# A kernel whose instruction order comes from a planner: the planner is given other transfer times, other mode-change times and a new table of keys

## The chip, the cores and the metric

The kernel runs on one core of one Trainium2 chip. The metric is the device time of one execution in microseconds (us), the median of several executions; lower is better. The engines are named as in the profile: PE is the matmul engine, PEld its weight loads, DVE the vector engine, ACT the scalar engine, POOL the GpSimd engine, SP the engine that issues most DMAs.

## The reference, cut to what matters

Two steps, in float32 (the weights may arrive as float64): a gated linear attention with a complex decay for 4 batches x 8 heads, 768 steps, head size 48, and a feed-forward layer with a softplus on its output.

```python
mag = np.sqrt(a_re * a_re + a_im * a_im)
scale = np.minimum(mag, 0.999) / (mag + 1e-06)
for t in range(S):                     # 768 steps, per batch and head
    S_re, S_im = ar * S_re - ai * S_im + k_t v_t^T, ar * S_im + ai * S_re
    y[:, :, t] = q_t @ S_re
x = y.transpose(0, 2, 1, 3).reshape(3072, 384)
h = x @ w_in                           # 384 -> 2048
g = np.maximum(h, 0.0) + np.log1p(np.exp(-np.abs(h)))
out = g @ w_out                        # 2048 -> 384
```

## The kernel before

**Attention.** The recurrence is done in chunks of 128 steps. The 24 chunks (6 time groups x 4 batches) are prepared in 14 slices: the first time group has one slice for each batch, every later group two slices of two batches. `pre` turns the decays of a slice into a running log magnitude and a running angle: on ACT logarithms and exponentials (one function table) and arctangent, sine and cosine (another table, and each change of table is an ACT_TABLE_LOAD from line 1031), on DVE products, and for the first time group the running sums as matmuls (L596). L668 and L670 then rotate keys and queries by cosine and sine. `chunk` moves the rotated block by four DMAs from one place in SBUF to another, into the tile qk (L717, L721), computes scores in 32-row pieces (L787), masks them on DVE (L791), adds the part of the carried state (L820) and the part within the chunk (L823), splits the result into a high and a low part in xt (L832 on ACT or L831 on DVE, then L833), and updates the state (L736 transposes, L743 and L745 copies, L859 matmuls, L871).

**Feed-forward.** `moe` takes one time group (512 tokens) at a time. For each of 16 blocks f of the inner size it runs nine matmuls into h (L898: three blocks of the input size, each as high x high, low x high, high x low), the softplus on ACT (L903, L904, L905) and DVE (L914, for the first group L908), the split of g (L916 on DVE or L917 on ACT, and L918), and two blocks later nine matmuls into the three accumulators o (L934). In the first group the second product is done with unsplit float32 weights (L931, three matmuls). The weights are loaded as 16 tiles raw_wi and raw_wo (L392, 768 KB each), converted from float64 words on DVE (L402, L405, L409) and split (L416 to L419).

**Order.** Nothing is scheduled by hand. Every task is entered with an engine, an assumed duration, its inputs and outputs, its buffers and a key (a due time). `Planner.order` plays the program through once: whenever an engine is free, it takes the ready task with the lowest key whose buffers are free. ACT tasks that need the other function table are put back by `tpen`, PE tasks in the other matmul mode (32-row pieces against full 128 rows) by `mpen`, and some ACT or DVE tasks may go to the other engine. When PE has nothing ready before the first feed-forward result, a filler matmul on the identity matrix is put in (L972). What the planner emits is each engine's instruction order; at run time every engine runs its list strictly in that order and waits where an input is missing. The keys come from the table K (base keys for each slice, chunk, weight and time group, and `nudge`, which shifts single tasks).

The lines on which the planner's clock of a DMA rests:

```python
if e == "SP":
    dma_free = max(dma_free, now + dur + 0.65) + t.nbytes / 330e3
    t.end = dma_free + 2.0
```

Of the kernel before, what the change touches and what calls it, by code (L numbers as in the profile page):

```python
# [21 lines left out]
P = 128  # L22
B, H, S, D = 4, 8, 768, 48
# [3 lines left out]
NI = DM // P  # L27
# [7 lines left out]
QT = 32  # L35
NQ = P // QT
# [52 lines left out]
class Task:  # L89
    __slots__ = ("eng", "dur", "fn", "key", "idx", "deps", "outs", "bufs", "tab", "nbytes", "left", "ready", "end", "alt", "mode")  # L90

    def __init__(self, eng, dur, fn, key, idx, tab, nbytes, mode=0):
        self.mode = mode
        self.eng, self.dur, self.fn, self.key, self.idx, self.tab, self.nbytes = eng, dur, fn, key, idx, tab, nbytes
        self.deps, self.outs, self.bufs, self.end = set(), [], [], 0.0
        self.alt = {}


class Planner:
    WIN = 3.4133  # L100
    FREE = 0.2
    SWITCH = (0.13, 0.095)
# [27 lines left out]
    def add(self, eng, dur, fn, key, r=(), w=(), tab=None, nbytes=0, mode=0):  # L130
        t = Task(eng, dur, fn, key, len(self.tasks), tab, nbytes, mode)
# [17 lines left out]
    def order(self, filler, until, gate):  # L149
# [44 lines left out]
        while done < n:  # L194
            for x in [x for x in ends if x[0] <= now]:
# [3 lines left out]
                for b in t.bufs:  # L199
                    users[b] = users.get(b, b.users) - 1  # L200
                    if users[b] == 0:
                        freed.append((t.end + self.FREE, b))
# [12 lines left out]
            for e in engines:  # L215
# [25 lines left out]
                if best is None and e == "PE" and ends and gate.end and not until.end:  # L241
                    t = Task("PE", FILL, filler, 0, -1, None, 0)
                    free[e] = now + self.array(now, t.dur + (self.SWITCH[0] if mode else 0.0))
# [59 lines left out]
class Prog:  # L303
# [165 lines left out]
    def pre(self, si):  # L469
# [60 lines left out]
        for j, w in enumerate((ca, sa)):  # L530
            def load(j=j):
# [6 lines left out]
            add("SP", 0.45, load,  # L538
                k + 0.1 * j, w=w, nbytes=8 * W * P)
# [139 lines left out]
    def chunk(self, si, c):  # L679
# [44 lines left out]
        for y in range(2):  # L724
            add("SP", 0.62, lambda y=y: heads(y), at(), r=rs, w=[(room, y)], nbytes=2 * D * NI * 1024)
        for y in range(2):
            add("SP", 0.62 if y else 1.4, lambda y=y: shared(y), at(), r=rs, w=[(room, 2 + y)], nbytes=2 * D * 1024)
# [23 lines left out]
        if not last and turned:  # L751
# [21 lines left out]
            add("SP", 2.0, back, at("state"), r=[kd], w=[k2], nbytes=5 * NQ * NI * 2 * QT * P)  # L773
# [366 lines left out]
    def tokens(self):  # L1140
# [73 lines left out]
        -16.338, 5181.86, 176.442, 1628.366, 68.743, 2476.615, 12057.262, 8932.26, 4865.317, 9147.526,  # L1214
        5423.692, 9290.079, 7158.223, 2244.123,
    ],
    "turn": [
        1592.16, 14330.158, 926.506, 1114.172, 2002.13, 8009.243, 7280.747, 7229.777, 2074.974, 18289.305,
        16766.682, 6503.433, 8105.153, 20021.708,
    ],  # L1220
    "tail": [
        226.025, 7990.761, 6717.881, 21069.729, 17662.929, 591.778, 3489.081, 3529.209, 2603.006, 18343.569,
        4472.776, 15471.677, 5298.621, 9447.507,
    ],
    "chunk": [
        -5948.126, 4596.693, 15086.453, 18259.591, 4231.75, 278.86, 1826.896, 2584.494, 518.594, 19365.021,
        1532.72, 14660.162, 6114.859, 22685.821, 7987.101, 4607.589, 20075.365, 7820.913, 15476.253,
        15113.712, 5780.716, 3707.156, 9835.409, 9278.805,
    ],
    "state": [  # L1230
        -17713.56, -25296.17, -5912.358, -1072.654, 80.456, 83.211, 122.678, 99.685, 129.906, 130.2, 154.062,
        147.079, 239.946, 176.388, 309.671, 460.52, 627.645, 901.311, 1502.438, 1822.573, 5296.098, 16265.588,
        19931.86, -586.874,
    ],
    "wgt": [
        13.204, 635.646, 440.261, 16753.966, 17898.824, 3564.011, 16258.655, 1674.662, 16642.242, -12846.499,
        710.902, 8004.565, 9718.573, 17872.114, 15509.821, 13690.111,
    ],
    "low": [
        3706.381, 13481.854, 4674.202, 518.67, 12581.252, 18757.155, -457.641, 127.016, 9766.312, 7691.499,  # L1240
        10533.41, 1633.717, 889.978, 19008.362, 16824.551, 16699.959,
    ],
    "moe": [
        51.097, 100.548, 355.358, 850.441, 4520.98, 22694.101,
    ],
    "step": [
        2.766, 4.919, 22.222, 144.776, 1126.208, 24756076.64,
    ],
    "seen": 22461.439,
    "seenstep": 0.268,  # L1250
    "rlead": 7551.755,
    "xlead": -7696.933,
    "vlead": -2102.967,
    "backlog": 1.748,
    "mpen": 0.622,
    "altpen": 0.065,
    "tpen": 1.84,
    "table": 1.3,
    "nudge": {
# [87 lines left out]
```

## Time and profile before

| | us |
|---|---|
| median of 3 executions | 575.77 |
| lowest and highest | 575.57, 577.8 |
| profiled execution: span from first to last instruction | 573.5 |
| PE busy | 543.3 (95%) |
| DVE busy | 438.9 (77%) |
| ACT busy | 422.9 (74%) |
| POOL busy | 5.7 (1%) |

The profile gives the span of one execution and not that execution's own full time; the median stands 2.3 us above the span. "Busy" for PE means that some matmul is in flight. A wait is put down to what came last before it ended; "issue" is time for which the profile shows no releaser.

### The profile page before, as it was taken

The numbers are of one execution on the slowest core, as the hardware profiler recorded it, in microseconds if no ns is written. First come the engines' busy times: TensorE is split into PE (matmuls) and PEld (weight loads), VectorE is DVE, ScalarE is ACT, GpSimd is POOL, SyncE is SP. The second block draws the span as 40 slices with busy tenths as digits, with TensorE's granted clock in tenths as the row PEclk, the third lists the DMA queues.
The fourth block names the chain that finished last, engine by engine and source line by source line (L and its number), as shares of the span: only waits on it lengthen the run. The fifth ranks groups of instructions, "written<-read, shape, count | busy, mean of one in ns | idle before, by whom it ended". The sixth has DMA issues, their size and how long they took to land.

```text
span 573.5 us, 14092 instructions
## 1 busy us (share of the span) xinstructions
PE 543.3 (95%) x5902; PEld 430.8 (75%) x5902; DVE 438.9 (77%) x681; ACT 422.9 (74%) x728; POOL 5.7 (1%) x27
## 2 busy tenths in 40 slices
PE   0998899999989999999999999999999999999995
PEld 0987766566667888878878887878878888888874
DVE  6598799999787999988899896886987544444442
ACT  7972688878579899786795966774969899854442
POOL 3000000000000000000000000000000000000000
PEclk9999999999999999999999999999999999999998
DMA  8869930162644413457276338184076887210002
GB/s 312 361 163 286 404 149 0 39 188 56 155 156 106 148 32 98 158 135 230 55 183 194 99 95 234 25 219 137 17 183 199 264 249 224 74 56 0 0 2 58
DMA packets 50164, 82.36 MB, mean 144 GB/s; under 512 B 4400, under 2 KB 34352, under 8 KB 50096
## 3 DMA queue, kind: packets, MB, share of 16 engines
q1 hardware_dynamic: 49568, 81.15, 47.2%
q8 instruction: 47, 0.77, 0.6%
q10 hardware_dynamic: 528, 0.26, 0.2%
q14 instruction: 21, 0.17, 0.1%
HBM read 54.66 MB, written 7.86 MB: 109 GB/s over the span
## 4 chain that ended last, share of the span: by engine, by line
PE 82%; ACT 7%; DVE 5%; issue 3%; DMA 2%; SPq 0%; DVEq 0%; ACTq 0%
PE h L898 32%; PE o L934 25%; PE o L931 7%; PE att L787 5%; PE att L820 3%; PE att L823 3%; PE o L972 3%; PE att L859 2%; DMA x<-dense_dram 2%; ACT L1031 1%; PE att L736 1%; DVE lt L914 1%; PE y L823 1%; ACT t L628 0%; ACT t L632 0%
## 5 line engine op out<-in xcount | busy, mean ns | idle before, releaser
L898 PE MATMUL h<-xt,wi 128*128 128x512 f32 x864 | 220.8, 402 | 1.1 <-DVE lt L914 0.9
L898 PEld LDWEIGHTS h<-xt,wi 128*128 128x128 f32 x864 | 160.0, 188 | 42.8 <-issue 3.9
L934 PE MATMUL o<-gh,wo 128*128 128x512 f32 x480 | 160.9, 396 | 0.0
L914 DVE SCALAR_TENSOR_TENSOR lt<-h,lt 128x512 f32<-128x512 f32 x80 | 54.7, 688 | 77.0 <-ACT lt L905 76.7
L903 ACT ACTIVATE lt<-h 128x512 f32<-128x512 f32 x96 | 56.5, 592 | 74.1 <-PE h L898 70.6
L934 PEld LDWEIGHTS o<-gh,wo 128*128 128x128 f32 x480 | 90.1, 188 | 21.6 <-issue 0.8
L934 PE MATMUL o<-gl,wo 128*128 128x512 f32 x240 | 94.3, 393 | 0.0
L905 ACT ACTIVATE lt<-lt,fixed 128x512 f32<-128x512 f32 x96 | 68.7, 719 | 1.6
L904 ACT ACTIVATE lt<-lt 128x512 f32<-128x512 f32 x96 | 59.9, 628 | 1.9
L918 DVE TENSOR_TENSOR gl<-lt,gh 128x512 fp32r<-128x512 f32 x80 | 54.6, 688 | 2.9 <-ACT gh L917 1.4
L934 PEld LDWEIGHTS o<-gl,wo 128*128 128x128 f32 x240 | 45.1, 188 | 10.1
L931 PE MATMUL o<-gf,raw_wo 128*128 128x512 f32 x96 | 43.7, 594 | 0.0
L1031 ACT ACT_TABLE_LOAD x30 | 38.5, 1283 | 0.5
L791 DVE TENSOR_TENSOR a<-att,mask 128x512 f32<-128x512 f32 x48 | 30.9, 682 | 9.3 <-PE att L787 9.2
L787 PE MATMUL att<-qk 96*32 96x96 f32 (+3 forms) x1536 | 33.3, 234 | 4.6 <-issue 4.6
L575 DVE TENSOR_TENSOR_SCAN t<-hold,t 128x384 f32<-128x384 uint8 x40 | 36.1, 945 | 0.7
L787 PEld LDWEIGHTS att<-qk 96*32 96x32 f32 x1536 | 29.7, 110 | 9.1 <-issue 7.3
L917 ACT ACTIVATE gh<-lt 128x512 fp32r<-128x512 f32 x30 | 18.7, 628 | 16.5 <-DVE lt L914 15.8
L931 PEld LDWEIGHTS o<-gf,raw_wo 128*128 128x128 f32 x96 | 17.8, 189 | 17.2 <-issue 15.8
L972 PE MATMUL o<-ident 128*128 128x128 f32 x196 | 25.9, 279 | 0.0
L916 DVE TENSOR_SCALAR gh<-lt 128x512 fp32r<-128x512 f32 x50 | 21.2, 425 | 5.8 <-PE o L934 2.5
L972 PEld LDWEIGHTS o<-ident 128*128 128x128 f32 x196 | 23.8, 193 | 0.9 <-issue 0.6
(102 smaller groups left out, 678.1 us busy)
## 6 DMA issues: line engine op xcount, KB each, us to landing
x<-dense_dram SPq DMA_DIRECT2D x20, 768.0 KB, 6.6
qk<-x SPq DMA_DIRECT2D x48, 288.0 KB, 4.1
raw_wo<-w_out_dram SPq DMA_DIRECT2D x8, 768.0 KB, 11.2
raw_wi<-w_in_dram SPq DMA_DIRECT2D x8, 768.0 KB, 9.5
seen<-w_in_dram SPq DMA_DIRECT2D x16, 384.0 KB, 3.9
seen<-w_out_dram SPq DMA_DIRECT2D x16, 384.0 KB, 4.3
v<-vpad_dram SPq DMA_DIRECT2D x24, 224.0 KB, 4.0
qk<-x SPq DMA_DIRECT2D x48, 96.0 KB, 3.8
```

Of the source, the lines that this page charges most:

```text
L575: V.tensor_tensor_scan(out()[:, s], self.hold, inc()[:, s], 0.0, ALU.mult, ALU.add)
L787: PE.matmul(psc()[QT * u : QT * (u + 1), hh * P + f : (hh + 1) * P], q[:, h, CH + f : CH + f + QT], q[:, h, f:CH], start=True, stop=True)
L898: PE.matmul(h()[:, :n], w()[:, q, i, fs], xt()[:, x, i], start=k == 0, stop=k == 3 * NI - 1)
L903: add("ACT", a1(n) - 0.04, lambda: A.activation(tv(), h(), AF.Abs), k, r=[h], w=[t])
L904: add("ACT", a1(n), lambda: A.activation(tv(), tv(), AF.Exp, scale=-1.0), k, w=[t], tab="log")
L905: add("ACT", a1(n, 1), lambda: A.activation(tv(), tv(), AF.Ln, bias=self.one), k, w=[t], tab="log")
L914: add("DVE", d1(n), lambda: V.scalar_tensor_tensor(tv(), h(), 0.0, tv(), ALU.max, ALU.add), k, r=[h], w=[t])
L918: add("DVE", d1(n), lambda: V.tensor_tensor(gl(), tv(), gh().bitcast(F32), ALU.subtract), k, r=[t, gh], w=[gl])
L931: PE.matmul(acc[m]()[:, :n], v, gt[0](), start=f == 0, stop=f == NF - 1)
L934: PE.matmul(acc[m]()[:, :n], w()[:, wq, f % 2, ms], x(), start=f == 0 and q == 0, stop=f == NF - 1 and q == 2)
L972: self.nc.tensor.matmul(self.acc0[0]()[:, :P], self.ident, x, start=True, stop=True)
L1031: nc.scalar.preload_act_table_set(TABLES[table])
```

## The change

The planner's clock is given other numbers, and the table K other keys. The tasks, their buffers and their arithmetic are the same. Line numbers after the class `Planner` are one lower than before (L717 becomes L716), since two lines of constants went.

- A DMA begins 1.4948 us after its issue instead of 0.65, and its data is ready 0.43 us after its bytes have passed instead of 2.0. Its rate is 370 x 1.011 GB/s instead of 330, and for the four DMAs into qk 220 x 1.011 x 0.992 GB/s.
- The first matmul after a change of mode costs 0.2626 us more in one direction and 0.08366 in the other, instead of 0.13 and 0.095. A change of mode is put back by 4.06 instead of 0.622, a change of function table by 0.15 instead of 1.84.
- A buffer is free 0.047 us after its last use instead of 0.2.
- `parts` is stored with a task and read by nothing.

```diff
-    FREE = 0.2
-    SWITCH = (0.13, 0.095)
...
-                        freed.append((t.end + self.FREE, b))
+                        freed.append((t.end + K["free"], b))
...
-                        dur += self.SWITCH[t.mode]
+                        dur += K["switch"][t.mode]
...
                 if e == "SP":
-                    dma_free = max(dma_free, now + dur + 0.65) + t.nbytes / 330e3
-                    t.end = dma_free + 2.0
+                    rate = t.rate * K["rate"] * (K["shuffle"] if t.rate < 300e3 else 1.0)
+                    dma_free = max(dma_free, now + dur + K["begin"]) + t.nbytes / rate
+                    t.end = dma_free + K["land"]
...
-            add("SP", 0.62, lambda y=y: heads(y), at(), r=rs, w=[(room, y)], nbytes=2 * D * NI * 1024)
+            add("SP", 0.62, lambda y=y: heads(y), at(), r=rs, w=[(room, y)], nbytes=2 * D * NI * 1024, rate=220e3)
...
 K = {
     "head": [
-        -16.338, 5181.86, 176.442, 1628.366, 68.743, 2476.615, 12057.262, 8932.26, 4865.317, 9147.526,
+        1234.0, 873.0, 78833.0, 14843.0, 86.2, 10514.0, 5881.0, 2424.0, 13176.0, 5466.0, 1848.0, 3422.0,
...
-    "backlog": 1.748,
-    "mpen": 0.622,
-    "altpen": 0.065,
-    "tpen": 1.84,
-    "table": 1.3,
+    "backlog": 1.903737,
+    "mpen": 4.06,
+    "altpen": 0.18,
+    "tpen": 0.15,
+    "table": 1.2956,
+    "switch": [0.2626, 0.08366],
+    "rate": 1.011,
+    "begin": 1.4948,
+    "land": 0.43,
+    "free": 0.047,
+    "shuffle": 0.992,
```

What this does to the order is shown at three places.

SP, around the transfers of the third and fourth chunk of the first time group; before, qk_547 and qk_635 are those two chunks, raw_wi and raw_wo are weight tiles, x_717 is the input of the first slice of the second time group.

```order
L721 DMA qk_416<-x_121 96x1x256
L392 DMA raw_wi_463<-w_in_dram 128x1536
L392 DMA raw_wo_495<-w_out_dram 128x1536
L717 DMA qk_547<-x_128 96x1x768 x2
L721 DMA qk_547<-x_128 96x1x256 x2
L717 DMA qk_635<-x_128 96x1x768 x2
L721 DMA qk_635<-x_128 96x1x256 x2
L392 DMA raw_wi_690<-w_in_dram 128x1536
L536 DMA x_717<-dense_dram 128x2x768 x2
```

After, qk_411 is the second chunk, qk_440 the third, qk_603 the fourth, and x_684 is what x_717 was.

```order
L716 DMA qk_440<-x_127 96x1x768 x2
L720 DMA qk_440<-x_127 96x1x256 x2
L716 DMA qk_411<-x_121 96x1x768
L391 DMA raw_wi_545<-w_in_dram 128x1536
L720 DMA qk_603<-x_127 96x1x256
L716 DMA qk_603<-x_127 96x1x768
L720 DMA qk_603<-x_127 96x1x256
L716 DMA qk_603<-x_127 96x1x768
L535 DMA x_684<-dense_dram 128x2x768
L391 DMA raw_wi_715<-w_in_dram 128x1536
```

Two weight loads stood ahead of both chunks' transfers; now none stands ahead of the third chunk and one ahead of the fourth.

ACT, around the sine and cosine of the third and fourth slice of the first time group (t_152 and t_160 before, each with a table load on either side):

```order
L1031 ACT_TABLE_LOAD
L631 ACTIVATE t_152<-t_152 128x384
L632 ACTIVATE t_152<-t_152,fixed 128x384
L1031 ACT_TABLE_LOAD
L616 ACTIVATE x_128<-sum_3_0_368 128x3x128 x2
L743 ACTIVATE kt_442<-att_91 128x3x2x48
L745 ACTIVATE kt_442<-att_91 128x3x32
L1031 ACT_TABLE_LOAD
L631 ACTIVATE t_160<-t_160 128x384
L632 ACTIVATE t_160<-t_160,fixed 128x384
```

After, the same slices are t_142 and t_153:

```order
L615 ACTIVATE x_127<-sum_3_0_369 128x3x128
L1030 ACT_TABLE_LOAD
L630 ACTIVATE t_142<-t_142 128x384
L631 ACTIVATE t_142<-t_142,fixed 128x384
L630 ACTIVATE t_153<-t_153 128x384
L631 ACTIVATE t_153<-t_153,fixed 128x384
L1030 ACT_TABLE_LOAD
L615 ACTIVATE x_127<-sum_3_0_369 128x3x128
```

Both slices now share one stay in the other table. Over the whole program that runs, ACT has 28 table loads at that line, before 30.

PE, ahead of the first scores of the second time group; before, x_717 is that slice, h and o the feed-forward of the first time group:

```order
L931 MATMUL o_905<-gf,raw_wo_144 128x512
L898 MATMUL h<-xt_545,wi_1097 128x512 x9
L898 MATMUL h<-xt_545,wi_1149 128x512 x9
L736 MATMUL att_93<-ident,x_717 128x128 x3
L736 MATMUL att_91<-ident,x_717 128x128 x3
L736 MATMUL att_92<-ident,x_717 128x128 x3
L931 MATMUL o_205<-gf,raw_wo_144 128x512
L931 MATMUL o_903<-gf,raw_wo_144 128x512
L931 MATMUL o_905<-gf,raw_wo_144 128x512
L736 MATMUL att_91<-ident,x_717 128x128 x3
```

There follow a state product and then the first scores, behind 13 blocks of h and 10 of o. After:

```order
L897 MATMUL h<-xt_583,wi_943 128x512 x9
L735 MATMUL att_91<-ident,x_684 128x128 x3
L930 MATMUL o_196<-gf,raw_wo_855 128x512
L930 MATMUL o_896<-gf,raw_wo_855 128x512
L930 MATMUL o_898<-gf,raw_wo_855 128x512
L897 MATMUL h<-xt_583,wi_1079 128x512 x9
L735 MATMUL att_93<-ident,x_684 128x128 x3
L930 MATMUL o_196<-gf,raw_wo_855 128x512
L930 MATMUL o_896<-gf,raw_wo_855 128x512
L930 MATMUL o_898<-gf,raw_wo_855 128x512
L786 MATMUL att_92<-qk_1087 32x128
```

The first scores of the second time group (qk_1087) now stand behind 10 blocks of h and 8 of o, and ahead of that state product.

Counted over the whole list, PE has the same instructions: 98 fillers (91 ahead of the first h before and 93 after; 7 and 5 behind it) and 94 changes of mode in both.

## Rows read from the trace of the kernel before

**Rows 1.** The first line of the page.
```profile
span 573.5 us, 14092 instructions
```

**Rows 2.** Busy time by stretch: us, then PE, PEld, DVE, ACT, POOL, PEclk, DMA share, GB/s.
```profile
65.00:150.00 85.00, 85.00 (x659) 55.16 (x662) 81.48 (x113) 68.11 (x108) 0.00 (x0) 1.00 0.38 118
150.00:185.00 35.00, 32.34 (x436) 25.28 (x426) 28.99 (x45) 29.34 (x52) 0.00 (x0) 1.00 0.45 128
185.00:567.00 382.00, 381.51 (x3995) 308.88 (x3993) 279.49 (x439) 282.23 (x482) 0.00 (x0) 1.00 0.44 125
```

**Rows 3.** What PE waited for: us in total, times, longest us.
```profile
PE sum L596 <- DVE t L566: 14.5, 1, 14.5
PE att L787 <- issue: 4.6, 2, 2.6
PE att L736 <- DVE x L670: 1.7, 1, 1.7
PE att L823 <- issue: 1.5, 1, 1.5
PE att L736 <- ACT kt L745: 0.6, 1, 0.6
```

**Rows 4.** Timeline of PE at the end of the first stage: start us, us, instruction, wait.
```profile
59.79 0.99 PE L787 MATMUL att<-qk 96*32 96x32 f32 x40 [2.61 <-issue]
...
65.06 4.43 PE L898 MATMUL h<-xt,wi 128*128 128x512 f32 x18
```

**Rows 5.** Timeline of ACT: a table load between the third and fourth slice.
```profile
39.07 1.28 ACT L1031 ACT_TABLE_LOAD   x1
```

**Rows 6.** Timeline of DVE: the rotations of the first four chunks.
```profile
27.89 0.16 DVE L605 COPY car<-sum 128x3 f32<-128x3 f32 x1 [2.18 <-ACT x L616]
...
37.85 0.95 DVE L670 TENSOR_TENSOR x<-x,t 128x768 f32<-128x768 f32 x1
...
42.16 0.96 DVE L670 TENSOR_TENSOR x<-x,t 128x768 f32<-128x768 f32 x1
```

**Rows 7.** Timeline of SP's DMA issues in the same stretch.
```profile
39.77 0.83 SPq L392 DMA_DIRECT2D raw_wi<-w_in_dram  x1
...
45.47 2.01 SPq L717 DMA_DIRECT2D qk<-x  x2
```

**Rows 8.** DMAs issued at 33.6, 46.3, 50.2 and 51.4: KB each, us to landing.
```profile
qk<-x SPq DMA_DIRECT2D x1, 288.0 KB, 3.6
...
qk<-x SPq DMA_DIRECT2D x1, 288.0 KB, 9.2
...
raw_wi<-w_in_dram SPq DMA_DIRECT2D x1, 768.0 KB, 7.8
...
x<-dense_dram SPq DMA_DIRECT2D x1, 768.0 KB, 8.7
```

**Rows 9.** The chain that ended last: start us, us, what.
```profile
35.05 2.87 PE o L972 x24
...
42.79 0.67 PE att L859 x48
...
73.15 2.57 PE o L931 x6
75.73 2.09 PE h L898 x9
```

**Rows 10.** Timelines of DVE and SP: first softplus result, rotation of the fifth chunk, its transfer.
```profile
69.81 0.67 DVE L908 SCALAR_TENSOR_TENSOR gf<-h,lt 128x512 f32<-128x512 f32 x1
...
109.33 0.94 DVE L670 TENSOR_TENSOR x<-x,t 128x768 f32<-128x768 f32 x1
...
110.30 0.58 SPq L717 DMA_DIRECT2D qk<-x  x1
```

**Rows 11.** Groups by line: out<-in, shapes, xcount | busy us, mean ns | idle before.
```profile
L405 DVE SCALAR_TENSOR_TENSOR bits_wi<-raw_wi,bits_wi 128x768 int32<-128x768 int32 x8 | 7.6, 950 | 0.0
L402 DVE TENSOR_SCALAR bits_wi<-raw_wi 128x768 int32<-128x768 int32 x8 | 4.4, 551 | 0.0
```

More of the change, by code (lines that the diff above doesn't have):

```diff
@@ L89, with __init__ @@
 class Task:
-    __slots__ = ("eng", "dur", "fn", "key", "idx", "deps", "outs", "bufs", "tab", "nbytes", "left", "ready", "end", "alt", "mode")
-    def __init__(self, eng, dur, fn, key, idx, tab, nbytes, mode=0):
-        self.mode = mode
+    __slots__ = ("eng", "dur", "fn", "key", "idx", "deps", "outs", "bufs", "tab", "nbytes", "left", "ready", "end", "alt", "mode", "parts", "rate")
+    def __init__(self, eng, dur, fn, key, idx, tab, nbytes, mode=0, parts=1, rate=370e3):
+        self.mode, self.parts, self.rate = mode, parts, rate
         self.eng, self.dur, self.fn, self.key, self.idx, self.tab, self.nbytes = eng, dur, fn, key, idx, tab, nbytes
@@ L128, in array, with add @@
                 return now - start
-    def add(self, eng, dur, fn, key, r=(), w=(), tab=None, nbytes=0, mode=0):
-        t = Task(eng, dur, fn, key, len(self.tasks), tab, nbytes, mode)
+    def add(self, eng, dur, fn, key, r=(), w=(), tab=None, nbytes=0, mode=0, parts=1, rate=370e3):
+        t = Task(eng, dur, fn, key, len(self.tasks), tab, nbytes, mode, parts, rate)
         self.tasks.append(t)
@@ L242, in order @@
                     t = Task("PE", FILL, filler, 0, -1, None, 0)
-                    free[e] = now + self.array(now, t.dur + (self.SWITCH[0] if mode else 0.0))
+                    free[e] = now + self.array(now, t.dur + (K["switch"][0] if mode else 0.0))
                     t.end = free[e]
@@ L536, in load @@
                     nc.sync.dma_start(region(j)[:, :, o : o + w], src[:, :, o : o + w])
-            add("SP", 0.45, load,
-                k + 0.1 * j, w=w, nbytes=8 * W * P)
+            add("SP", 0.85 if si == j == 0 else 0.45, load,
+                k + 0.1 * j, w=w, nbytes=8 * W * P, parts=2 if si == j == 0 else 1)
         for c in range(m):
@@ L724, in chunk @@
         for y in range(2):
-            add("SP", 0.62, lambda y=y: heads(y), at(), r=rs, w=[(room, y)], nbytes=2 * D * NI * 1024)
+            add("SP", 0.62, lambda y=y: heads(y), at(), r=rs, w=[(room, y)], nbytes=2 * D * NI * 1024, rate=220e3)
         for y in range(2):
-            add("SP", 0.62 if y else 1.4, lambda y=y: shared(y), at(), r=rs, w=[(room, 2 + y)], nbytes=2 * D * 1024)
+            add("SP", 0.62 if y else 1.4, lambda y=y: shared(y), at(), r=rs, w=[(room, 2 + y)], nbytes=2 * D * 1024, rate=220e3)
         if not last and not turned:
@@ L771, in back @@
                     nc.sync.dma_start(k2()[QT * q : QT * (q + 1)].rearrange("a (u n) -> a u n", u=NQ), src[q])
-            add("SP", 2.0, back, at("state"), r=[kd], w=[k2], nbytes=5 * NQ * NI * 2 * QT * P)
+            add("SP", 2.0, back, at("state"), r=[kd], w=[k2], nbytes=5 * NQ * NI * 2 * QT * P, parts=NQ)
         am = []
@@ L1213 @@
     "head": [
-        -16.338, 5181.86, 176.442, 1628.366, 68.743, 2476.615, 12057.262, 8932.26, 4865.317, 9147.526,
-        5423.692, 9290.079, 7158.223, 2244.123,
+        1234.0, 873.0, 78833.0, 14843.0, 86.2, 10514.0, 5881.0, 2424.0, 13176.0, 5466.0, 1848.0, 3422.0,
+        14829.0, 27806.0,
     ],
     "turn": [
-        1592.16, 14330.158, 926.506, 1114.172, 2002.13, 8009.243, 7280.747, 7229.777, 2074.974, 18289.305,
-        16766.682, 6503.433, 8105.153, 20021.708,
+        841.0, 8899.0, 15364.0, 126.0, 12635.0, 2144.0, 5457.0, 2591.0, 5814.0, 630.0, 9435.0, 16621.0,
@@ L1220 @@
+        20992.0, 19812.0,
     ],
     "tail": [
-        226.025, 7990.761, 6717.881, 21069.729, 17662.929, 591.778, 3489.081, 3529.209, 2603.006, 18343.569,
-        4472.776, 15471.677, 5298.621, 9447.507,
+        110.0, 28414.0, 18751.0, 5829.0, 10058.0, 6574.0, 70693.0, 344.0, 751.0, 79142.0, 3964.0, 10539.0,
+        2519.0, 43479.0,
     ],
     "chunk": [
-        -5948.126, 4596.693, 15086.453, 18259.591, 4231.75, 278.86, 1826.896, 2584.494, 518.594, 19365.021,
-        1532.72, 14660.162, 6114.859, 22685.821, 7987.101, 4607.589, 20075.365, 7820.913, 15476.253,
@@ L1228 @@
-        15113.712, 5780.716, 3707.156, 9835.409, 9278.805,
+        17817.0, 4755.0, -136.0, 160.0, 12091.0, 313.0, 7490.0, 11010.0, 21206.0, 15589.0, 4840.0, 28652.0,
+        18646.0, 3281.0, 10068.0, 15892.0, 18086.0, 18548.0, 15917.0, 20584.0, 11621.0, 5290.0, 13476.0,
+        15776.0,
     ],
     "state": [
-        -17713.56, -25296.17, -5912.358, -1072.654, 80.456, 83.211, 122.678, 99.685, 129.906, 130.2, 154.062,
-        147.079, 239.946, 176.388, 309.671, 460.52, 627.645, 901.311, 1502.438, 1822.573, 5296.098, 16265.588,
@@ L1233 @@
-        19931.86, -586.874,
+        -29618.0, -36450.0, -17971.0, -1296.0, 80.0, 86.0, 132.0, 97.0, 129.0, 127.0, 161.0, 180.0, 357.0,
+        189.0, 789.0, 578.0, 1061.0, 850.0, 2467.0, 1696.0, 3800.0, 440.0, 2237.0, 6192.0,
     ],
     "wgt": [
-        13.204, 635.646, 440.261, 16753.966, 17898.824, 3564.011, 16258.655, 1674.662, 16642.242, -12846.499,
-        710.902, 8004.565, 9718.573, 17872.114, 15509.821, 13690.111,
+        -1297.0, 732.0, 11332.0, 10373.0, 233.0, -3610.0, 8304.0, 74952.0, 10375.0, 17830.0, 1664.0, 4711.0,
@@ L1238 @@
+        7111.0, 11931.0, 115.0, 15366.0,
     ],
     "low": [
-        3706.381, 13481.854, 4674.202, 518.67, 12581.252, 18757.155, -457.641, 127.016, 9766.312, 7691.499,
-        10533.41, 1633.717, 889.978, 19008.362, 16824.551, 16699.959,
+        9824.0, 1502.0, 8370.0, 8324.0, -148.0, 16617.0, 2170.0, 103.0, 12085.0, 79142.0, 48497.0, 7472.0,
+        50.0, 18518.0, 824.0, 6186.0,
     ],
     "moe": [
-        51.097, 100.548, 355.358, 850.441, 4520.98, 22694.101,
+        51.0, 101.4, 510.0, 1224.0, 9677.0, 48527.0,
@@ L1245 @@
     ],
     "step": [
-        2.766, 4.919, 22.222, 144.776, 1126.208, 24756076.64,
+        2.8, 5.1, 24.3, 164.0, 2268.0, 8534.0,
     ],
[L1249 to L1253, printed above, removed]
-    "backlog": 1.748,
-    "mpen": 0.622,
-    "altpen": 0.065,
-    "tpen": 1.84,
-    "table": 1.3,
-    "nudge": {
[19 rows of a table removed]
+    "seen": 3882.0,
+    "seenstep": 9160.0,
+    "rlead": -2017.0,
+    "xlead": -1130.0,
+    "vlead": -16095.0,
+    "backlog": 1.903737,
```

36 rows, old and new, of the table K are left out of this document.

## The prediction

> **What bounds the kernel now.** The views were read in this order: busy time by stretch, PE's waits, then the timelines of the first 65 us engine by engine, the landing times of the transfers there, and the chain that ended last. The reader is to see that PE is the bound and that its list contains almost the same work after the change, so that only its waits can move. From 65 to 150 us PE is never idle, from 150 to 185 us it lacks 2.66 us, from 185 to 567 us 0.49 us [rows 2]. Ahead of 65 us it waits 14.5 us for its first input, and then 4.6 + 1.7 = 6.3 us more [rows 3]. Beside this, 91 fillers stand there, 12 of them (24 records, two for each) in 2.87 us, 0.24 us each [rows 9]. The order after has the same matmuls, the same 98 fillers and the same 94 changes of mode. So the new prices for a change of mode bring nothing by themselves, and all that can be won is the 6.3 + 2.7 + 0.5 = 9.5 us of waits behind the first matmul. The sum is made against the span of 573.5 us [rows 1]; the median of the runs, 575.77 us, stands 2.27 us above it, and I carry that difference over.
>
> **The first stage (until the first h, 65.06 us [rows 4]).** The last thing that PE waits for is the fourth chunk's block in qk, until 59.79 us; from there to the first h it takes 5.3 us [rows 4]. Its rotation ends at 42.16 + 0.96 = 43.1 us [rows 6], its transfers are issued from 45.5 us on, directly behind two weight loads and the third chunk's transfers [rows 7]. A qk transfer that was issued at 33.6 us landed 3.6 us later, one that was issued at 46.3 us took 9.2 us [rows 8]: 5.6 us of queue. After, no weight load stands ahead of the third chunk's transfers and one ahead of the fourth's, issued several us earlier.
>
> I walked along after's lists with the durations of before's timelines, each step at the later of its engine's last end and its inputs. The rotations of the first two chunks end 3.4 us earlier, as DVE no longer stands behind a copy that waits 2.18 us for ACT [rows 6] and ACT has one operation less ahead. The third ends at 37.2 us instead of 38.8. The fourth ends at about 45.5, 2.4 us later than before, because ACT now does both slices' sines before it returns to the other table; two loads of 1.28 us each fall away [rows 5], but what the fourth slice needs from the first table comes after. That does not matter for the transfers: SP was busy with the third chunk until 45.5 us before, and is free at that time now. So the fourth chunk's transfers are issued from 45.5 us again, at about 1 us each [rows 7], and the last lands 3.6 us after its issue, at about 53 us. PE reaches that score at 55.5 us, because the third chunk's y, 16 fillers (3.8 us) and the second chunk's y stand ahead of it. Behind it come the score, the masks, y, the split, and now also a state product under the split: 5.3 us as before, and 0.5 us for the half of the score that was done earlier then. First h at 61.3 us: **-3.8 us**. Bounds: if the waits go entirely and only the two added fillers stand against it, 65.06 - 6.3 + 0.5 = 59.3 us, or -5.8; if they all stay, +0.5. I take the walk, which lies between.
>
> [...]
>
> **Behind the first h.** Two fillers fewer: **-0.5 us** (2 x 0.24). The 1.5 us wait of L823 is a y that PE reaches straight after its own score, while DVE masks; after, a state product of 0.7 us [rows 9] stands between, so 0.8 is left. The 0.6 us of L736 is the fourth transpose in a row, with three banks for them [rows 3]; after, no more than three stand in a row there. Together **-1.3 us**, bounds 0 and -2.7 (all idle time of that stretch [rows 2]).
>
> **The fifth chunk, the added wait.** Its score stands behind 10 blocks of h, 8 of o, two transposes and 5 fillers: 10 x 2.09 + 8 x 2.57 + 0.8 + 1.2 = 43.5 us behind the first h, at 104.8 us (a transpose is three matmuls, each at about half a filler's 0.24) [rows 9]. Before it stood 13 us later: three blocks of h, two of o, two fillers, two transposes and a state product more. Its block must be ready so much earlier. DVE needs, from the first L908 to the end of that rotation, 69.81 to 110.27 = 40.5 us [rows 10] with nearly no gap. After, two L908, three L402, two L405 and one each of L409, L419, L561 and L668 are missing there: at 0.55 us for L402 and up to 0.95 us for the others [rows 11] some 8 us, a little less than the sum of the durations since neighbours overlap. First L908 4.75 us behind the first h as before, at 66.0, so the rotation ends at 98.5. Four issues and a landing, 3 + 3.6 us [rows 7, 8], on an empty queue: 105.1 us, **+0.3 us**. Queued behind a waiting score on PE are two blocks of h and everything after, so the wait would be paid in full. Bounds: 0, and +9.0 if DVE's idle time at the start does not shrink with the first stage (3.8) and the landing takes 9.2 instead of 3.6 (5.6). I take the value near 0, because nothing but that chunk is in the queue there: before, too, the first of these transfers was issued at 110.30, alone [rows 10].
>
> **At nothing:** two table loads, 2.6 us of ACT [rows 5]; ACT is idle 5.7 of 35 and 100 of 382 us in the later stretches [rows 2]. DVE gets 20 copies that ACT did, some 10 us at the 0.55 us of the nearest row [rows 11]; from 185 us on it is idle for 102 us [rows 2]. Between 65 and 150 us that cover is not there, DVE being busy for 81.5 of 85 us; what it would cost is the second rival. Behind the last matmul nothing moves.
>
> Sum: -3.8 - 0.5 - 1.3 + 0.3 = -5.3 us; span 568.2, time **570.5 us**.
>
> **Rivals.**
> (1) DVE takes over. If DVE cannot start its work behind the first h earlier, since it is full from 65 to 150 us [rows 2], PE waits there for L908 and the conversions, and the 3.8 us come back: 574.3 us. For it: DVE had about 1 us of air in that stretch. Against it: its work ahead of the first L908 is the same, and the shorter first stage takes its idle time away, not its work. The same number comes out if the new transfer times are no truer than the old and the waits merely move.
> (2) Slower: the score of the fifth chunk, moved 13 us forward on an engine that cannot pass it, stands and waits for its block. The price is the upper bound, 9.0 instead of 0.3: 579.2 us. It decides from a wait of 5.6 us on, where the gain is gone. For it: three weight loads stand on SP directly ahead of that chunk. Against it: by the walk they are issued before 70 us, and even in the full queue such a load had landed 7.8 to 8.7 us after its issue [rows 8], some 20 us before that chunk is ready.
> (3) Nearly all waits go: -6.3 - 2.7, 566.8 us. For it: the planner's DMA clock now has queueing and a slower rate for qk, which is what the waits at 53 and 59.8 us come from. Against it: a plan on any clock leaves some.
>
> **Chances.** Forecast 0.45, rival (1) 0.22, (2) 0.13, (3) 0.20. A measurement of this kernel can tell a difference of 0.5%, 2.9 us, from none: below 572.9 is faster, above 578.6 slower. Faster: 0.38 of the forecast's 0.45 and all of (3), 0.58. Same: 0.07 + 0.22 = 0.29. Slower: 0.13. The range leaves out (2) and the lower part of (3): 566.0 to 577.0. The forecast's own range is 568 to 573.
>
> **What would show it.** The first h at 61.3 us (59.3 to 64); the fourth chunk's transfers landing within 5 us of issue; no "issue" wait at L787 ahead of it (now L786) above 1 us; the fifth chunk's first score at 104 to 106 us, with the rotation ending near 98.5; PE's idle time from 150 to 185 us near 1.3 us. The forecast is wrong if the first h comes after 64 us, or if PE's idle time between the first h and the end is over 4 us; then the row of waits names which rival it was.

## The result: 570.3 us after, 575.9 us before

| | before | after |
|---|---|---|
| median of 4 executions, us | 575.91 (575.57 to 577.8) | 570.33 (568.67 to 570.65) |
| ratio of the times | | 0.9888, 95% interval 0.9865 to 0.9912 |
| span and time of the profiled execution, us | 573.5 | 567.0 and 568.67 |
| first h, us | 65.06 | 58.88 |
| first h to the end of the span, us | 508.4 | 508.1 |

The forecast was 570.5 us. A second measurement of the changed kernel gave 569.9 us (0.9893, interval 0.9869 to 0.9916). Nearly all of the gain lies ahead of the first h: it comes 6.2 us earlier, and what follows takes as long as before. In the profile of the second measurement (e10, span 568.9) the first h comes 5.9 us earlier, at 59.17, and what follows takes 509.7 us, 1.3 longer.

Busy time by stretch, after, in the columns of [rows 2]:

```profile
65.00:150.00 85.00, 85.00 (x762) 53.56 (x764) 82.51 (x116) 65.53 (x105) 0.00 (x0) 1.00 0.42 138
150.00:185.00 35.00, 33.60 (x368) 26.56 (x358) 31.23 (x52) 29.51 (x53) 0.00 (x0) 1.00 0.45 126
185.00:567.00 382.00, 375.31 (x3922) 302.86 (x3920) 280.09 (x443) 267.66 (x456) 0.00 (x0) 1.00 0.44 126
```

The last row holds 6.2 us of the end, where PE is done. PE idles 1.4 us from 150 to 185 us (2.66 before) and still not at all from 65 to 150. All that PE waited for (us in total, times, longest), against [rows 3]:

```profile
PE sum L595 <- DVE t L565: 13.8, 1, 13.8
PE h L897 <- DVE lt L913: 0.8, 3, 0.4
PE att L822 <- issue: 0.7, 1, 0.7
PE att L858 <- DVE a L790: 0.3, 1, 0.3
```

The 6.3 us of waits between the first matmul and the first h are gone. PE's timeline there, against [rows 4] (the first h is the L897 row; L786 at 54.12 is the fourth chunk's score; 32 records of L971 are 16 fillers):

```profile
48.34 1.18 PE L822 MATMUL y<-a,v 128*32 128x128 f32 x32
49.45 3.84 PE L971 MATMUL o<-ident 128*128 128x128 f32 x32
53.22 1.08 PE L822 MATMUL y<-a,v 128*32 128x128 f32 x32
54.12 1.31 PE L786 MATMUL att<-qk 96*32 96x128 f32 x64
...
58.88 4.44 PE L897 MATMUL h<-xt,wi 128*128 128x512 f32 x18
```

The steps ahead of it: DVE's third and fourth rotation, against [rows 6], SP's issues of the fourth chunk's transfers, against [rows 7], and the landing of the last of them (KB each, us to landing), against [rows 8]:

```profile
36.05 0.96 DVE L669 TENSOR_TENSOR x<-x,t 128x768 f32<-128x768 f32 x1
...
44.22 0.95 DVE L669 TENSOR_TENSOR x<-x,t 128x768 f32<-128x768 f32 x1
```

```profile
45.31 0.57 SPq L720 DMA_DIRECT2D qk<-x  x1
45.93 0.60 SPq L716 DMA_DIRECT2D qk<-x  x1
46.58 1.63 SPq L720 DMA_DIRECT2D qk<-x  x1
48.26 0.60 SPq L716 DMA_DIRECT2D qk<-x  x1
```

```profile
qk<-x SPq DMA_DIRECT2D x1, 288.0 KB, 3.8
```

The last lands at 48.26 + 3.8 = 52.1 us, two us before PE reaches the score. The fifth chunk, against [rows 10]: first softplus result, rotation of its first half, score:

```profile
63.72 0.68 DVE L907 SCALAR_TENSOR_TENSOR gf<-h,lt 128x512 f32<-128x512 f32 x1
...
94.45 0.95 DVE L669 TENSOR_TENSOR x<-x,t 128x768 f32<-128x768 f32 x1
```

```profile
103.14 1.33 PE L786 MATMUL att<-qk 96*32 96x128 f32 x64
```

No wait stands at that score.

### The profile page after: what moved, and what is told of

It is laid out like the page before. It is cut to its first block, busy times and chain, and to the rows that moved or that the text cites. A ratio compares the mean times of both kernels' runs of the same rounds, so it can differ in the third digit from the quotient of the medians.

```text
span 567.0 us, 14093 instructions
## 1 busy us (share of the span) xinstructions
PE 545.1 (96%) x5902; PEld 431.3 (76%) x5902; DVE 447.7 (79%) x701; ACT 408.6 (72%) x706; POOL 5.7 (1%) x27
## 4 chain that ended last, share of the span: by engine, by line
PE 88%; ACT 5%; DVE 4%; issue 1%; DMA 1%; SPq 0%; ACTq 0%
PE h L897 34%; PE o L933 26%; PE o L930 7%; PE att L786 5%; PE o L971 4%; PE att L819 3%; PE att L822 3%; PE att L858 3%; PE sum L595 1%; PE att L735 1%; DMA x<-dense_dram 1%; ACT lt L902 1%; ACT L1030 1%; PE y L822 1%; ACT lt L903 1%
## 5 line engine op out<-in xcount | busy, mean ns | idle before, releaser
L897 PE MATMUL h<-xt,wi 128*128 128x512 f32 x864 | 219.6, 401 | 1.0 <-DVE lt L913 0.8
L897 PEld LDWEIGHTS h<-xt,wi 128*128 128x128 f32 x864 | 159.7, 188 | 45.1 <-issue 3.7
L786 PE MATMUL att<-qk 96*32 96x128 f32 (+3 forms) x1536 | 32.6, 234 | 0.0
L786 PEld LDWEIGHTS att<-qk 96*32 96x32 f32 x1536 | 29.9, 110 | 3.4 <-issue 2.9
L915 DVE TENSOR_SCALAR gh<-lt 128x512 fp32r<-128x512 f32 x61 | 25.7, 424 | 3.3
L971 PE MATMUL o<-ident 128*128 128x128 f32 x196 | 26.0, 283 | 0.0
L971 PEld LDWEIGHTS o<-ident 128*128 128x128 f32 x196 | 24.0, 196 | 0.6 <-issue 0.2
L667 DVE TENSOR_TENSOR x<-x,t 128x768 f32<-128x768 f32 x24 | 22.3, 952 | 2.0 <-ACT t L630 2.0
```

What stands on the lines that cost most here:

```text
L786: PE.matmul(psc()[QT * u : QT * (u + 1), hh * P + f : (hh + 1) * P], q[:, h, CH + f : CH + f + QT], q[:, h, f:CH], start=True, stop=True)
L897: PE.matmul(h()[:, :n], w()[:, q, i, fs], xt()[:, x, i], start=k == 0, stop=k == 3 * NI - 1)
L971: self.nc.tensor.matmul(self.acc0[0]()[:, :P], self.ident, x, start=True, stop=True)
```

## The experiments

All experiments are timed against the kernel before on the same chip. "Code waits" are the waits for "issue" ahead of the first h; e1 and e2 show why they have that name. The line numbers in a row of an experiment are those of its own file, the names tell what it is.

| kernel | first h | code waits ahead of it | median | ratio (95% interval) |
|---|---|---|---|---|
| before | 65.06 | 2.0 + 2.6 | 575.1 to 575.5 | 1 |
| e1 before, two loads behind | 61.30 | 1.5 | 574.17 | 0.9977 (0.9956 to 0.9998) |
| e2 after, two loads ahead | 61.17 | 1.0 + 1.1 + 0.5 | 570.62 | 0.992 (0.9891 to 0.9949) |
| e3 after, 35 fillers out | 59.87 | 1.4 | 569.86 | 0.9897 (0.9873 to 0.9921) |
| e4 after, masks early | 60.77 | 2.6 | 579.14 | 1.0071 (1.0049 to 1.0094) |
| e5 head of after, rest of before | 59.04 | 0.3 | 578.43 | 1.0041 (1.0021 to 1.0061) |
| e6 head of before, rest of after | 65.50 | 0.7 + 2.6 | 578.86 | 1.0063 (1.0041 to 1.0086) |
| e7 e1 and an empty queue | 59.58 | none | 573.27 | 0.9964 (0.9945 to 0.9983) |
| e8 after, table loads apart | 59.96 | 0.3 | 571.35 | 0.9931 (0.9903 to 0.9959) |
| e9 before, wide fillers | 66.30 | 2.9 | 575.16 | 0.9998 (0.9977 to 1.0019) |
| e10 after again | 59.17 | none | 569.9 | 0.9893 (0.9869 to 0.9916) |
| e11 after, wide fillers | 59.90 | 1.8 | 569.67 | 0.9894 (0.987 to 0.9917) |
| e12 after, copies on the engines of before | 59.29 | none | 586.7 | 1.0191 (1.0166 to 1.0215) |

In the diffs, numbers are tasks of the planner, and `move(out, tasks, after)` puts tasks behind another one in the planned order.

**e1, weight loads behind the fourth chunk (kernel before).** 819 and 815 load wi2 and wo1, 172 is the fourth chunk's last transfer, 820 wi2's first conversion, 164 the third chunk's split.

```diff
+        move(out, (819, 815), 172)
+        move(out, (820,), 164)
```

> The kernel before, with one thing of the change: its two weight loads that stood ahead of the third chunk's transfers into qk (tiles wi2 and wo1) are issued behind the fourth chunk's, and the first conversion of wi2 on DVE stands behind the third chunk's masks. PE's list is untouched, all fillers stay. Queue theory: the waits of 2.0 and 2.6 us for the third and fourth chunk's score (L787) go, the third chunk's transfers land about 4 us after issue instead of 9; first h at 60.4 to 61 us instead of 65.06, time 571 to 572. Rival (the order as a whole is what gained): the wait only moves, to the conversions of the two late tiles or to a mask behind them; first h at 64 us or later, time 574 to 576.

The profiled execution went nearly as the queue theory said: first h at 61.30, span 569.7. But one wait stayed, inside the fourth score:

```profile
53.84 0.67 PE L798 MATMUL att<-qk 96*32 96x128 f32 x24
56.03 0.99 PE L798 MATMUL att<-qk 96*32 96x32 f32 x40 [1.52 <-issue]
...
61.30 4.49 PE L909 MATMUL h<-xt,wi 128*128 128x512 f32 x18
```

The chunk's four transfers were issued by 45.8 us; the last two took 4.7 to 5.9 us, by this view of their line:

```profile
L732 SPq DMA_DIRECT2D qk<-x x2: 602/1018/1435, 44.4 to 45.8; - x2
...
DMA to landing us min/median/max: 4.7/5.3/5.9
```

All of them lay there by 51.7 us, over four us before PE went on. So PE did not wait for them. The rows of the DMA queues give the other candidate: the queue "instruction", read here as the one that brings PE's program (e2 gives the grounds). In the half microsecond from 53.5 us one packet of it began (packets, MB, share of 16 engines):

```profile
q1 hardware_dynamic: 30, 0.18, 94.8%
q8 instruction: 1, 0.02, 13.9%
```

The median gained only 0.2%, though, and the profiled execution is one of the two fastest: of twelve the two with a mean granted clock of 0.999 took 570.8 and 571.4 us, the two with the longest times, 576.5 and 577.0, had 0.989 and 0.992. What pulled the clock down in those, their lists of times don't show; in e3, e4 and e9 the granted clock was 0.69, 0.50 and 0.50 over five us, behind five us in which PE was busy for 3.39, 1.58 and 2.08.

**e2, weight loads ahead of the second scored chunk (kernel after).** 829 and 849 load wi3 and wi5, 112 is a transfer of the chunk before.

```diff
+        move(out, (829, 849), 112)
```

> The changed kernel, with two weight loads (tiles wi3 and wi5) issued ahead of the transfers of the chunk that is scored second, as before; nothing else differs. Queue theory: those transfers land 5 to 6 us later (about 9 instead of 4 us after issue), PE waits about 3.4 us for that chunk's score, first h at 62.3 us instead of 58.9, time 573 to 574. Rival (PE had room, or the loads and the transfers take turns): first h within 0.5 us of 58.9, time 570 to 571.

The transfers took 7.1 to 8.0 us instead of about 4, and the first h came 2.3 us later. The time did not follow: 570.62 us is what the rival expected, and the intervals of the two ratios overlap. PE waited three times for "issue", once in the middle of a y that reads no transfer:

```profile
46.16 0.98 PE L796 MATMUL att<-qk 96*32 96x64 f32 x38 [1.02 <-issue]
...
50.55 0.43 PE L832 MATMUL y<-a,v 128*32 128x128 f32 x8 [1.06 <-issue]
...
57.28 0.44 PE L796 MATMUL att<-qk 96*32 96x32 f32 x9 [0.48 <-issue]
```

Counted along PE's list, the waits stand behind the 475th, the 603rd and the 730th record. In the kernel before, the two waits stand behind the 602nd and the 730th, although other work stands there. The step is 128 matmul records, with their weight loads 256 instructions, and the packet of the instruction queue is 0.02 MB. Over the whole execution before, 47 such packets passed, against 11,804 records of PE (5,902 matmuls and as many weight loads), some 251 for each:

```profile
q8 instruction: 47, 0.77, 0.6%
```

By this step, the 251 records for a packet and the name of the queue, such a packet is read here as the next block of PE's program, its code, and these waits as waits for it. In the kernel before they were 2.0 and 2.6 us.

**e3, no fillers (kernel after).**

```diff
+        h = next(k for k, t in enumerate(out) if t.idx == 980)
+        out = [t for k, t in enumerate(out) if t.idx >= 0 or not 211 <= k < h]
```

> The changed kernel without the 35 fillers that stand on PE between 40 us and the first h (8.2 us of PE time); nothing else differs. Theory A (the fillers only cover waits for masks on DVE and for the fourth chunk's transfers): PE is idle about 7 us more in the first stage, first h at 58.6 to 59.0 us, time within 1 us of the changed kernel's 570.3. Theory B (the list of PE itself sets the first h, since PE waited nowhere behind its first matmul): first h at 57 us or earlier, time 568.5 or less. Theory C: the granted clock falls where the fillers are missing, and the first h comes later than 59.5 us.

Theory A: the time is that of the changed kernel, and the longest wait in place of the fillers is for a mask on DVE:

```profile
PE y L824 <- DVE a L792: 4.6, 3, 3.1
```

The first h is 1.0 us late although its fillers are gone: the first sum came 0.8 us later (14.6 instead of 13.8), and a code wait of 1.4 us stands at the 730th record, which is now a matmul of the state product. Theory C is seen too: behind five us in which PE was busy for 3.39 the granted clock is 0.69 (columns as above):

```profile
45.00:50.00 5.00, 3.39 (x159) 2.88 (x146) 5.00 (x8) 1.56 (x4) 0.00 (x0) 1.00 0.71 174
50.00:55.00 5.00, 2.65 (x61) 2.67 (x64) 5.00 (x8) 1.34 (x2) 0.00 (x0) 0.69 0.86 256
```

**e4, masks early (kernel after).** A list of tasks is replayed in place of a stretch of the order. DVE's tasks in it, before the edit and after (121 and 123, 178 and 180 are the masks; the fillers and ACT's order are not shown):

```diff
-145, 821, 806, 822, 164, 807, 121, 123, 804, 808, 810, 178, 180, 811, 126, 812, 183
+145, 821, 806, 121, 123, 822, 164, 807, 178, 180, 804, 126, 810, 183, 811, 812, 808
```

> The changed kernel with the masks of the third and fourth scored chunk taken on DVE ahead of weight conversions, 11 of the 22 fillers ahead of the first h left out, and the softplus of the first two blocks ahead of the next slice's logarithms on ACT; the same operations otherwise. By walking along the lists the first h comes at 56.4 us instead of 58.9. Theory A (PE's start sets the end, DVE follows): the 2.4 us stay to the end, time 568. Theory B (DVE, full from 44 to 150 us, is the second bound): the first h is early all the same, but PE then waits about 2 us for L907 or for weights behind it, and the time is 570 to 571.

Neither theory: PE came to its 730th record early, before its code, and stood 2.6 us at a y whose inputs were there; the first h came 1.9 us later than in the changed kernel, not 2.5 earlier. Behind it, the third L921 came late on DVE, PE stood 4.9 us, and the clock fell:

```profile
58.22 1.08 PE L836 MATMUL y<-a,v 128*32 128x128 f32 x32 [2.56 <-issue]
...
81.48 6.81 PE L911 MATMUL h<-xt,wi 128*128 128x512 f32 x18 [4.90 <-DVE gf L921]
```

1.9 + 4.9 and some 2.4 us of slow clock (18 h in 6.81 us instead of 4.44; the granted clock was 0.50 from 80 to 85 us) are nearly all of the 9.3 us between the spans, 576.3 and 567.0.

**e5 and e6, heads exchanged.** The order is replayed from a list: one kernel's tasks up to the first h, then the other's order for what is left.

```diff
-        return out
+        return splice(self.tasks, home, PLAN, next(t for t in out if t.idx < 0))
```

> All that the changed kernel issues ahead of its first h, in its order on every engine, and then the order of the kernel before for everything that is left. Theory A (the whole gain is made ahead of the first h): first h at 58.9 us, PE's waits behind it as before (3.2 us), time 570 to 571. Theory B (the gain hangs on the plan as a whole): the old order does not fit the new start, PE's waits behind the first h grow to 6 us or more, time 573 or more.

> The other way round: all that the kernel before issues ahead of its first h, then the order of the changed kernel. Theory A (the whole gain is made ahead of the first h): first h at 65 us, time 574 to 575.5. Theory B (the plan as a whole): PE's waits behind the first h fall to 2 us or less and the time to 573 or less, or they grow and it is above 576.

Both are slower than before, as theory B has it. The head keeps its time (59.04 and 65.50), but the seam costs more than it gives. In e5 DVE's list goes on with a conversion of a weight tile whose load the other head had issued early; here it comes late, and L1042 (L908 of before) stands behind it:

```profile
65.15 0.56 DVE L536 TENSOR_SCALAR bits_wo<-raw_wo 128x768 int32<-128x768 int32 x1 [5.26 <-DMA raw_wo<-w_out_dram]
```

```profile
PE h L1032 <- DVE gf L1042: 8.3, 1, 8.3
```

In e6 the same wait of PE takes 2.2 us. Behind the seam e5 waits 1.5, 0.5 and 0.5 us, little as in [rows 3]. So the head keeps its gain in another plan, but the time keeps it only where DVE's order behind it fits. As a measure of the parts the pair is inconclusive.

**e7, the queue empty at the time of the code (kernel before).** 212 loads x_5 and waits for the fourth chunk's transfers.

```diff
+        move(out, (212, 819, 815), 172)
+        move(out, (820,), 164)
```

> The first experiment once more (kernel before, the two weight loads behind the fourth chunk's transfers), and the next slice's input x_5 put ahead of those loads: it must wait for its buffer until the fourth chunk's transfers have landed, so no load is queued between 47 and 51 us and the queue is short when PE's next block of code is fetched. PE's list is untouched. Theory A (PE's waits for 'issue' are its code, which stands in the same DMA engines behind data; they come at every 128th matmul record whatever that matmul reads): no wait of over 0.5 us at the 730th record in the fourth score, first h at 59.5 to 60.3 us, and the code's packet passes over 2.3 us before PE reaches that record. Theory B (PE waits there for the chunk's transfers): the 1.5 us stay, first h at 61.3 us.

Theory A: the code's packet began at 51.2 us, 0.6 us after PE had begun the block ahead of it and 3.2 us before it came to the 730th record, and the fourth score runs through. The loads were late in turn, and DVE behind them, so that of the 5.5 us at the first h the median kept 2.1:

```profile
53.99 1.31 PE L798 MATMUL att<-qk 96*32 96x128 f32 x64
...
61.70 4.22 PE L909 MATMUL h<-xt,wi 128*128 128x512 f32 x17 [1.65 <-DVE xt L844]
68.90 2.36 PE L909 MATMUL h<-xt,wi 128*128 128x512 f32 x9 [1.42 <-DVE gf L919]
```

**e8, table loads apart (kernel after).** A list of tasks is replayed as in e4. ACT's order in it: sines of the third and fourth slice (108, 109), the fourth's log step (82), two copies.

```diff
-108, 109, 82, 155, 157
+108, 82, 155, 157, 109
```

> The changed kernel with the sines of the third and fourth slice on ACT apart again: the fourth slice's logarithm-table step and the third chunk's two copies stand between them, so there are two table loads of 1.28 us more. The prediction put these loads at nothing. Theory A (nothing): first h within 0.4 us of 58.9, time within 1 us of 570.3. Theory B (sharing the table is part of the gain): the fourth rotation ends 2 to 3 us later, first h at 61 us or later, time 572 or more.

Between the theories: the first h came 1.1 us later, 0.2 of it at the first sum and 0.5 at a transpose that waited for the fourth rotation, and a wait of 1.0 us for L918 followed. The two loads were not free at the first h. The median lies 1.0 to 1.5 us above those of the changed kernel, but the intervals of the ratios overlap, so a cost in time is not shown.

**e9, wide fillers (kernel before).**

```diff
+            if t.idx < 0 and last is not None:
+                last.fn, last = wide, None
+                continue
...
+        self.nc.tensor.matmul(self.acc0[0]()[:, : 2 * P].rearrange("p (a b) -> p a b", a=2), self.ident,
+                              self.ident[:, None, :].to_broadcast([P, 2, P]), start=True, stop=True)
```

> The kernel before with every two neighbouring fillers on PE replaced by one of double width (same PE time, half the instructions; 98 fillers become 55). No transfer and no other instruction moves. Theory A (PE waits for blocks of its code, which end at the same record counts whatever stands there: 474, 602, 730): the waits move in the program to where those counts now fall, the 602nd record into the fillers behind the third score and the 730th into the y of the fourth chunk, and neither score has a wait inside. Theory B (PE waits there for the chunks' transfers): the waits stay where they were, after the first 2 records of the third score and the first 24 of the fourth. The sum of the two stays near 4 us under either, first h between 63 and 65.5 us.

Theory A in the places, though the wait is 2.9 us and not some 4. The third and fourth score run through, with their transfers untouched; the wait stands behind the 474th record, in the second score:

```profile
49.93 1.18 PE L799 MATMUL att<-qk 96*32 96x96 f32 x20 [2.92 <-issue]
...
56.84 1.33 PE L799 MATMUL att<-qk 96*32 96x128 f32 x64
...
60.29 1.31 PE L799 MATMUL att<-qk 96*32 96x128 f32 x64
```

PE came to the 602nd record late enough. The first h is later than expected; the granted clock was 0.50 from 50 to 55 us, right behind that wait.

**e10, the changed kernel again.** No edit.

> The changed kernel as it is, a second time, beside the others of this call: first h between 58.5 and 59.7 us (as its first sum comes at 13.4 to 14.6 us), no wait for issue over 0.5 us ahead of it, time 570.3 plus or minus 0.8.

As expected. The spread of the changed kernel's spans is 567.0 to 568.9 us over both measurements. In this execution the fourth score took 1.76 us instead of 1.31 around its 55th record, the 730th of the list: read here as a short wait for code that the profile counts as busy.

**e11, wide fillers (kernel after).** The edit of e9.

> The changed kernel with the same pairing of fillers. Its PE list has no wait for code ahead of the first h, so nothing is to be won there. Theory A (masks on DVE and the fourth chunk's transfers set the first h): first h within 0.5 us of the changed kernel's, time within 1 us of it. Theory B (the blocks of code still cost something that the profile hides, or the longer fillers overshoot): 1 us or more either way.

Theory A as to the time, but the first h came 1.0 us later than in the changed kernel (0.7 than in e10): PE came to its 730th record, now in the state product behind the y, earlier than its code and waited 1.8 us.

**e12, 44 copies on the engines of before (kernel after).** The order of the changed kernel is replayed as in e5. In the list a number above 10000 puts its task on the task's other engine, and these marks are those of the kernel before:

```diff
+        t.eng, t.fn = home[t.idx]
+        if x >= 10000:
+            t.eng, t.fn = next((e, a[1]) for e, a in t.alt.items())
```

> The changed kernel in its order, but the 44 copies and splits that the two kernels give to different engines (32 on ACT before and on DVE after, 12 the other way, all behind the first h) stand on the engine of the kernel before. The prediction put these moves at nothing. Theory A (nothing): the first h as before them, time within 1 us of the changed kernel. Theory B (the relief of ACT is part of what keeps the gain): PE's waits behind the first h grow by 1.5 us or more, time 572 or more.

Theory B, far beyond its bound: 16 us lost. PE waits 13.1 us behind its first matmul instead of 1.8, at many places, and its busy time rises from 545.1 to 551.1 us; what that rise consists of was not settled. The four largest waits:

```profile
PE h L1032 <- DVE lt L1048: 5.1, 4, 2.6
PE o L1068 <- ACT gh L1051: 2.1, 1, 2.1
PE att L954 <- DVE a L925: 1.6, 2, 1.4
PE h L1032 <- ACT xt L966: 1.2, 1, 1.2
```

## Why the prediction was right, and which of its steps was wrong

**The sum.** Span 568.2 and time 570.5 were forecast; the spans were 567.0 to 568.9 and the medians 570.33 and 569.9. The sign, the size and the place (ahead of the first h) are right. That the sum fits so closely is luck: ahead of the first h 6.2 us (5.9 in e10) were won instead of 3.8, behind it 0.3 (in e10 1.3 lost) instead of 1.5.

**First h, 61.3 forecast, 58.88 measured: mis-sized, and on a wrong cause.** The walk's steps on DVE and SP held: third rotation ends at 37.0 (37.2 forecast), fourth at 45.2 (45.5), transfers from 45.3 (45.5), last landing at 52.1 (53), 3.8 us after its issue, though the next load was issued 0.7 us behind it. The two steps on PE did not. PE reached the fourth chunk's score at 54.12 us (55.5 forecast), 0.7 of it from an earlier first sum, and went from there to the first h in 4.8 us (5.8 forecast): 12 records of fillers stand in that stretch, where before there were 28.

The cause was wrong at the step "the last thing that PE waits for is the fourth chunk's block in qk". The transfer with the next heads, issued at 46.3 with 9.2 us [rows 8], lay there at 55.5 us, and PE went on at 59.79 [rows 4]. That gap of 4 us stood in rows that the prediction quotes, and it read "issue" as a transfer. The other of the two waits in [rows 3] is this one of the kernel before, 128 records ahead:

```profile
53.05 1.33 PE L787 MATMUL att<-qk 96*32 96x96 f32 x62 [2.00 <-issue]
```

It ended when the last transfer of its chunk landed (issued at 44.3, 8.7 us), but it stands behind 2 of the 8 records of the chunk's first head, which one earlier transfer brings whole. In the kernel before a packet of code began in the quarter microsecond from 50.25 us and one in the quarter from 57.25:

```profile
q8 instruction: 1, 0.02, 32.0%
...
q8 instruction: 1, 0.02, 27.4%
```

These shares of 16 engines are 1.3 and 1.1 us of one. PE went on 2.8 and 2.5 us after they began, at 53.05 and 59.79. In the twelve such waits of the eight kernels in the table that have one of 0.4 us or more this distance is 2.2 to 2.8 us (1.3 to 1.5 from the packet's end), and the places are behind the records 474 or 475, 602 or 603, and 730, whatever stands there. e1, e4 and e9 exclude the transfers.

In the changed kernel packets began in the quarters from 46.25 and 52.25:

```profile
q8 instruction: 1, 0.02, 37.3%
...
q8 instruction: 1, 0.02, 28.2%
```

PE went on behind the records 603 and 730 at 49.1 and 55.0, 2.7 us later each time, with no wait of note. The first packet had come sooner: PE began the block ahead of it at 45.8 us before and 45.9 after, and the packet began 4.4 us later before, 0.4 us later after. The second was nearly as late as before (3.3 us instead of 4.2), but PE took 5.9 us over the block ahead of it instead of 3.9, as 16 fillers stand in that block. The planner knows nothing of code; that its order just covers both packets is luck too.

So the weight loads ahead did cost time, but by this reading through the code, whose packet came late with them queued (4.4 and 4.2 us after PE had begun the block ahead of it in the kernel before, 0.6 in e7), and not through qk. The gain of 6.2 us by measured terms: code waits 2.0 + 2.6, the wait of 1.7 us for a rotation (which no run isolates), 0.7 of an earlier first sum (which the prediction didn't have, and which scatters by 1.3 us over the kernels), less 0.5 for two fillers more; that is 6.5, and 0.3 stay unassigned. The lower bound of 59.3 us was missed by the first sum. What such a wait costs in the total is not shown one for one: e1 brought the first h 3.8 us forward and the median 1.0, e7 5.5 and 2.1, and e2 put it 2.3 us back and the median 0.3 to 0.7.

**Two fillers fewer and the waits from 150 to 185 us, -0.5 and -1.3: the second was right in size, not in cause.** PE idles 1.40 us there (near 1.3 forecast), and the 0.6 us of L736 are gone as forecast. But the 1.5 us at L823 were no mask: that wait stands in the middle of a y, and a packet of code began 2.4 us before it ended. The changed kernel waits 0.7 us (0.3 in e10) at the same place, so the 0.8 that was to be left there is a hit by luck. The two terms together did not arrive: from the first h to the end only 0.3 us were won. PE's idle time fell by 1.2 us, its busy time rose by 1.0. Short waits inside busy time, as in e10, may be part of it; this was not settled.

**Fifth chunk, +0.3: nothing.** Its rotation ended at 95.4 instead of 98.5, the score ran at 103.14 without a wait. The upper bound of 9.0 is a slip: its terms, 0.3 + 3.8 + 5.6, add up to 9.7, and rival (2) would have been at 579.9.

**At nothing: true of this plan, not of its parts.** 20 net copies on DVE and two table loads were put at nothing since an engine was idle enough. PE's waits in the changed kernel bear that out, but e12 shows what such a sum leaves out: the idle time must lie where the list needs it. With these copies put back the same order lost 16 us, and e8's two loads cost 1.1 us at the first h.

**The rivals.** (1), DVE takes over, did not happen in the changed kernel (82.51 us busy from 65 to 150 us, no wait); the "about 1 us of air" that spoke for it are 3.5 us in [rows 2]. It did happen in e4, e5 and e7, where the head was not matched behind. (2) did not happen. (3), nearly all waits go, describes the head.

## What to carry to other kernels

A wait for "issue" in the middle of a run of equal matmuls, whose inputs have landed, was read as a wait for code in all of these kernels (it ended 2.2 to 2.8 us after a packet of the instruction queue had begun): count the records between two such waits, and look when the packets of the instruction queue begin. Keep bulk loads out of the queue where an engine with many small instructions needs its next block: with them queued its packet began 4.4 and 4.2 us after the engine had begun the block ahead (kernel before), with them issued later 0.6 us (e7). And in a kernel of in-order lists, idle time of an engine covered an added operation only at the place where it stood (e12 lost 16 us): a part of such a plan cannot be priced or moved alone.

## What the hardware showed that was not expected

- PE's waits for "issue" stood in steps of 128 matmul records or just under (127.4 on average from the 730th to the 1,749th, behind both of which the kernel before waits); these places are read here as the ends of blocks of its code. Where PE waited at one, it went on 2.2 to 2.8 us after the packet began, and it stood up to 2.9 us. Counted on at that step, no packet but the last began more than some 20 records ahead of the block before its own, in the kernels before and after.
- Behind one such wait, the 2.9 us of e9, the granted clock was lower: PE was busy 2.08 of 5 us, and the five us behind ran at 0.50. In the kernel before, the waits of 2.0 and 2.6 us left it at 1.00, with PE busy 3.00 us from 50 to 55 us and 2.39 from 55 to 60. e9:

```profile
45.00:50.00 5.00, 2.08 (x98) 1.67 (x100) 3.09 (x4) 1.53 (x3) 0.00 (x0) 0.93 0.99 273
50.00:55.00 5.00, 5.00 (x36) 3.41 (x39) 2.90 (x4) 0.00 (x0) 0.00 (x0) 0.50 1.07 250
```

- A change between 32-row and 128-row matmuls shows as about 0.1 us on either side of nine matmuls into h (from their start to that of the next work 2.09 us alone, 2.19 and 2.29 with one and two changes next to them, in the kernel before from 186.41 and 207.58 us on); there were 94 changes in both kernels, so by itself it moved nothing.
